# Linear attention and a gated MLP on one core: softmax sums of two more tiles formed in down's rounds, wo's parts loaded and cast later, some loads reordered

## The chip, the cores and the metric

The kernel runs on one core of one Trainium2 chip. The metric is the device time of one execution in microseconds (us); lower is better. The engines are TensorE (PE, with its weight loads as PEld), VectorE (DVE), ScalarE (ACT), GpSimd (POOL) and SyncE (SP), each with a program of its own that it runs in order. SyncE, and ScalarE for a few, also issue DMAs; each DMA issue takes one of eight lanes in turn, so that an issue waits until the eighth DMA before it has landed. Everything is float32.

## The reference

`x` is 2048 x 1024. The output is `x + s * g`: `s` is linear attention with a learned feature map, `g` the silu of a gated MLP, both on the layernorm of `x`.

```python
xn = layernorm(x)
q, k, v = heads(xn @ wqkv)                     # 32 heads of 32
pq, pk  = q @ w_phi, k @ w_phi                 # per head
phi_q   = concat(softmax(pq), softmax(-pq))    # 64 features
phi_k   = concat(softmax(pk), softmax(-pk))
kv      = phi_k.T @ v                          # per head, over all rows
z       = phi_k.sum(rows)
o       = (phi_q @ kv) / (phi_q @ z + 1e-6)
s       = o @ wo
g       = silu((silu(xn @ w1) * (xn @ w3)) @ w2)     # hidden size 3584
out     = x + s * g
```

## The kernel before

Every large product is split twice. Each float32 operand becomes a high and a low part (`split`, L91: a cast on ScalarE, L93, then a subtraction on VectorE, L94), and three passes of matmuls (high x high, high x low, low x high) replace one. On top, blocks of 2 x 2 are multiplied by a scheme with seven products instead of eight (`ORDER`, L60: A11, A12, S2, S1, S3, S4, A22), which accumulate in three PSUM banks a, b and c. A bank is copied out between the products that add onto it, so a later product of the same bank waits for the copy: A11, S2, S3 and A22 share bank b.

The stages follow each other on TensorE:

- Gates and up (PE L667), to about 1117 us: layernorm, w1 and w3, h to DRAM (`h_d`).
- Heads (`heads` L938, PE L947), 1117 to 1450: k and v for the 16 row tiles as 8 pairs, once for each half of the columns (c = 0, 1). The operands `xoA`, `xoS` of a pair are loaded a pair ahead by `reload` (L630): seven loads of 512 KB. After S2 the pair before is added to kv (PE L908, tile `pkv`). Of each pair, `k` is copied from bank b after A11 (ACT L953), d0 after S2 (L964), d1 after S1 (L968); VectorE adds S3 and S4 (L972, L970). Beside this, one part of wo (128 x 512) is loaded (`wo_raw`, L1202), split (`wo_half`) and stored (`wo_d`, L1208) per pair by `wo_split`, at numbered steps j of the pair. Only TensorE's order is written by hand here; the other engines' orders come from the tile scheduler.
- Queries (c = 2; PE L1021), 1450 to 1602: phi_q, stored as `e_d` in DRAM.
- Down (PE L1420), 1602 to 2140: 56 rounds r, each of seven products (the step of a product is 7r + m), h @ w2 summed over kb = r // 8 into 16 slabs `acc`. Work is hung onto products by a table of steps (`pieces`).
- Output (PE L1564 `po`, L1583 `pm`), 2140 to 2356: for each row tile t, `attend` multiplies phi_q with kv (po), the result is cast to high and low parts (`oT`: ACT L1572, DVE L1573), and two halves of 24 matmuls each multiply it by wo (`wos`, and `late` for two of its 16 parts); then x g (DVE L1591) + x (POOL L1595), and the store (SP L1599).

From the last query pair on, all five engines run in the order in which the code is written.

The denominators of phi_q are needed as a factor on e (`scale`, L1397), before it is transposed (L1400) and used by `attend`. They come from products of e with z on GpSimd (`weighted`, L1333), sums over a head's features on VectorE (`summed`, L1336), a small matmul with `consts` that adds the two halves of features (`us`), and a reciprocal (L1369). For the tiles t < `EARLY` = 4 this happens in down's rounds 18 to 39, in eight parts (a tile's half each) 21 products apart: `load_part` (L1330, into a buffer in `room`), the product 12 products later and the sum 16 later, into `early_z`. For the tiles from 4 on it happens in the output loop, for tile t + 4 at step t: `z_products(t + 4)`, later `z_sums(t + 4, c)`, then `weigh`, `add_pairs`, `invert` and `factors` of t + 3 one step on. `z_sums` stands on VectorE between the subtractions of the two column halves that form oT's low parts:

```python
for c in range(2):
    if count:
        lows[c].pop(0)()
    if t + 4 >= EARLY:
        z_sums(t + 4, c)
```

`load_e` (L1389) loads a tile's e, `load_g` (L1549, L1550) the tile's gates g and its x (`xr`), all on SyncE. `B_LOADS` gives the pair and product of c = 2 at which w2's first eight pieces are loaded.

Of the kernel before, what the change touches and what calls it, by code (L numbers as in the profile page):

```python
# [17 lines left out]
P = 128  # L18
# [3 lines left out]
G = 8  # L22
NKB = NF // 4
EPS = 1e-5
PAD = 32


@with_exitstack
def tile_kernel(ctx: ExitStack, tc: tile.TileContext, x, wkT, wqT, wv, wphi, wo, w1, w3, w2, out):
# [104 lines left out]


    edge = [pool("edge_l", 1), pool("edge_r", 1, side="right")]
    edge[0].tile([P, 112], F, name="edge_l")
    edge[1].tile([P, 120], F, name="edge_r")
    misc = pool("misc", 1)
    small = pool("small", 2)  # L140
# [41 lines left out]
    ident = misc.tile([P, P], F, name="ident")  # L182
    consts = misc.tile([P, P], F, name="consts")
    eps_t = consts[:, 0:1]
    early_z = small.tile([P, 256 + PAD], F, name="early_z", bufs=1)[:, :256]

    def load_x(t, halves):
        for h in range(2):
# [132 lines left out]
        nc.sync.dma_start(raw_b[f], w1[f].rearrange("p (h k) n -> p h (k n)", h=2))  # L321
    for f in range(2):
        b_part(rws[f], f, 1)
    phi_raw = early_z.rearrange("p (g f) -> p g f", f=DH)
# [599 lines left out]

    pkv, out_now = None, []

    def kv_run(first, last, tiles):

        nonlocal pkv
        if first:  # L930
            pkv = ps.tile([P, 512], F, name="pkv", tag="kv", bufs=1)[:, :512 // 2]
            pkv = pkv.rearrange("p (m n) -> p m n", m=4)
            zsum.clear()
        for n, (e, v) in enumerate(tiles):
            z_add(e)
            kv(pkv, first and n == 0, last and n + 1 == len(tiles), e, v)

    def heads(first, last, apart, xo, wb, steps, pend):  # L938

        bank = {}  # L940
        for b, an, bn in ORDER:
            if b not in bank:
                bank[b] = ps.tile([P, 512], F, name=f"bank{b}", tag=f"bk{b}", bufs=BANKS[b])
            n = 0
            for k in range(4):
                for u, w in PASSES:
                    nc.tensor.matmul(bank[b], xo[an][:, u, k], wb[bn][:, w, k], start=an in ("A11", "A12", "S1") and n == 0,  # L947
                                     stop=LAST[b] == an and n == 11, skip_group_check=True)
                    n += 1
            pb, pv = bank[b], bank[b].rearrange("p (h d) -> p h d", d=DH)  # L950
            if an == "A11":
                k0 = work.tile([P, 512], F, name="k0", tag="w")
                nc.scalar.copy(k0, pb)  # L953
            elif an == "A12":
                nc.vector.tensor_add(k0, pb, k0)
                e0 = keys(k0, room_e())
            elif an == "S2":
                if pend:
                    kv_run(*pend)
                    if first:  # L960
                        out_now.extend(kv_out(0, pkv))
                v0 = room_v(0)
                d0 = v0
                nc.scalar.copy(d0, pv)  # L964
            elif an == "S1":
                v1 = room_v(1)
                d1 = v1
                nc.scalar.copy(d1, pv)  # L968
            elif an == "S3":
                nc.vector.tensor_add(d1, pv, d1)  # L970
            elif an == "S4":
                nc.vector.tensor_add(d0, pv, d0)  # L972
            else:
                if apart:
                    kv_run(first, False, [(e0, v0)])
# [104 lines left out]
    def query_heads(i, first, xo, wb, steps):  # L1080

        bank, rho = {}, small.tile([P, 2, 2, 16], F, name="rho")
        for b, an, bn in ORDER:
            pb = query_product(bank, b, an, bn, xo, wb)
            if an in ("A11", "S2", "S1"):
                t = work.tile([P, 512], F, name="q", tag="w")
                nc.scalar.copy(t, pb)
                if an == "A11":
                    q00 = t
                elif an == "S2":  # L1090
                    q01 = t
                else:
                    q11 = t
            elif an == "A12":
                nc.vector.tensor_add(q00, pb, q00)
                early = e_room()
                query_features(i, 0, 0, q00, rho, nc.gpsimd, early[:, 0])
            elif an == "S3":
                nc.vector.tensor_add(q11, pb, q11)
                query_features(i, 1, 1, q11, rho, nc.gpsimd, early[:, 1])  # L1100
            elif an == "S4":
                nc.vector.tensor_add(q01, pb, q01)
                late = e_room()
# [95 lines left out]
    def wo_split(c, k, j, halves):  # L1199
        if j == 0:  # L1200
            halves.append(work.tile([P, 512], F, name="wo_raw", tag="w"))
            nc.sync.dma_start(halves[0], wo[k * P:(k + 1) * P, c * 512:(c + 1) * 512])  # L1202
        elif j == 3:
            halves.extend(work.tile([P, 512], R, name="wo_half", tag="w") for _ in range(2))
            split(halves[1], halves[2], halves[0])
        elif j == 5:
            for u in range(2):
                nc.sync.dma_start(wo_d[c][k][:, u], halves[1 + u].bitcast(F))  # L1208

    in_order(ENG.PE)  # L1210
    B_LOADS = ((1, 5), (2, 5), (3, 5), (4, 5), (5, 2), (5, 5), (6, 2), (6, 5))
    NEXT = ({0: 2, 1: 3, 2: 4, 3: 5, 4: 6}, {0: 2, 1: 3, 2: 4, 3: 5, 6: 6}, {})
    for c in range(3):
        wbn, last = {}, c == 2
# [4 lines left out]
        for pos, i in enumerate(order):  # L1219
            nxt, end = {}, pos + 1 == len(pairs)  # L1220

            def steps():
                halves = []
                for j in range(7):
                    if not last:
                        wo_split(c, pos, j, halves)
                    if j == 0:
                        if pos in (3, 4) and not last:
                            wbn.update(fetch(3 + c, pos - 3))
                        if not end:  # L1230
                            nxt.update(reload(order[pos + 1]))
                    if last and (pos, j) in B_LOADS:
                        m = B_LOADS.index((pos, j))
                        load_b(0, m // 2, (m % 2,))
                    if end and j in NEXT[c]:
                        wbn.update(fetch(3 + c, NEXT[c][j]))
                    if last and pos + 2 == len(pairs) and j == 5:
                        ahead[0] = load_h(0, 0)
                    yield
# [21 lines left out]
        load_b(0, n)  # L1261

    wos, us, ezs = {}, {}, []
    EARLY, KEPT, gs = 4, 6, {}

    def load_wo(k):
        t = ring("wos")
# [3 lines left out]
    def gate(i, j):  # L1271
# [3 lines left out]
            nc.scalar.dma_start(g_d[t], slabs[:, m])  # L1275
        else:
            gs[t] = slabs[:, m]

    def slot_f(name):
        return flat(ring(name).bitcast(F))  # L1280
# [55 lines left out]
        nc.vector.tensor_reduce(of_half(dst, c), by_head(e), axis=AX.X, op=OP.add)  # L1336

    def weigh_early():
        nc.gpsimd.tensor_mul(early_z, early_z, w_all[:, :256])

    def add_early():
        us["early"] = ps.tile([P, 512], F, name="us", tag="kv", bufs=1)
        nc.tensor.matmul(us["early"][:, :256], consts, early_z, start=True, stop=True)

    def invert_early(k):
        u = us.pop("early") if k else us["early"]
        nc.vector.reciprocal(early_z[:, k * P:k * P + P], u[:, k * P:k * P + P])

    def z_products(t):
# [106 lines left out]
        pieces.setdefault(at_, []).append(do)  # L1456

    for n in range(2 * EARLY):
        at_ = 7 * 18 + 21 * n
        piece(at_, lambda n=n: load_part(n))  # L1460
        piece(at_ + 12, lambda n=n: weighted(er, er, n % 2))
        piece(at_ + 16, lambda n=n: summed(early(n // 2), er, n % 2))
    piece(at_ + 17, load_weights)
    piece(at_ + 30, weigh_early)
    piece(at_ + 33, add_early)
    piece(at_ + 35, lambda: invert_early(0))
    piece(at_ + 37, lambda: invert_early(1))
# [10 lines left out]
    for r, new in enumerate(steps):  # L1478
# [6 lines left out]
        if r == 4:  # L1485
# [1 line left out]
            room_z = rwp.tile([P, 2, D], F, name="room", tag="rw")  # L1487
            zb, er = room_z[:, 0], room_z[:, 1]
            w_all = er
        if r == 17:  # L1490
            load_z()
        if end:
            if i == 0:
# [4 lines left out]
                    load_wo(k)  # L1498
            elif 4 < i < 8:
                load_e(i - 4)  # L1500
        parts, bank = first, {}
        if r and new:
            gen2 = second_parts(*parts)
# [41 lines left out]
    def load_g(t):  # L1545
        if t < NT:
            if t not in gs:
                gs[t] = flat(quad("g", F).rearrange("p u k t -> p u (k t)"))
                nc.sync.dma_start(gs[t], g_d[t])  # L1549
            nc.sync.dma_start(xrs[t % 2], x[t * P:(t + 1) * P, :])  # L1550


# [46 lines left out]
        nc.sync.dma_start(out[t * P:(t + 1) * P, cs], gs[t][:, cs])  # L1599

    load_g(0)
    load_e(4)
    for c in range(2):
        attend(0, c, 1)[0]()
    prev, lows = None, []
    for t in range(NT):
        p, last = out_half(t, 0), t + 1 == NT
        if t + 5 < NT:
            load_e(t + 5)
        if 0 < t < 3:  # L1610
            gate(len(pairs) - 1, t - 1)
        for low in lows:
# [12 lines left out]
        if prev:  # L1625
            gate_mul(t - 1, 1, prev)
            gate_add(t - 1, 1, False)
            store_out(t - 1, 1)
        load_g(t + 1)
        gate_mul(t, 0, p)  # L1630
        if t + 3 >= EARLY:
            add_pairs(t + 3)
# [53 lines left out]
```

## Time and profile before

| | us |
|---|---|
| median of 3 runs | 2359.5 (2357.18 to 2361.13) |
| profiled execution, its own time | 2358.1 |
| its span, first to last instruction | 2356.3 |
| TensorE busy | 2325.3 (99%) |
| VectorE busy | 1819.5 (77%) |
| ScalarE busy | 888.9 (38%) |
| GpSimd busy | 255.4 (11%) |
| granted clock, mean | 0.998 |

A row of the timeline gives start and duration in us, the engine and line, the operation with output <- input, the count, and in brackets the idle time of the engine ahead of it with what ended that idle time. Idle time matters on TensorE, whose busy share is 99%; on another engine it costs nothing by itself. "SPq" and "PEld" are SyncE's DMA issues and TensorE's weight loads. A row of the wait list gives the engine and line that waited, what it waited for, the total, the number of times and the longest.

### The profile page before, as it was taken

The page shows a single profiled execution, that of the slowest core. Times are in us where ns is not written, and L with a number is a line of the kernel's source. Part 1 is how long each engine was busy: PE and PEld are TensorE (multiplying, and loading weights), DVE is VectorE, ACT ScalarE, POOL GpSimd, SP SyncE. Part 2 cuts the span into 40 slices and gives each one's busy share as a digit, 9 for nine tenths or more (in the row PEclk, how much of TensorE's full clock was granted, in tenths as well). Part 3 has the DMA queues.
Part 4 walks back from the last instruction along what each step waited for, and adds up shares of the span by engine and source line. Part 5 has one row for each costly group of instructions (what it writes and reads, how often), then busy time and mean ns, then how long its engine had stood idle before and what let it go on. Part 6 is the DMA issues. An engine that isn't in the chain of part 4 may idle for free.

```text
span 2356.3 us, 33840 instructions
## 1 busy us (share of the span) xinstructions
PE 2325.3 (99%) x12734; PEld 1901.6 (81%) x12734; DVE 1819.5 (77%) x2853; ACT 888.9 (38%) x1561; POOL 255.4 (11%) x212
## 2 busy tenths in 40 slices
PE   8999999999999999999999999999999999998999
PEld 6778877788888888888787887888888888886777
DVE  8878788885688888874677777778678888786884
ACT  6445444443345555543222222334433343352000
POOL 1000000000000000000000001331012222112652
PEclk9999999999999999999999999999999999999999
DMA  3456799997778888866978878996543554478863
GB/s 128 160 193 225 245 306 370 342 323 222 244 280 300 301 289 295 292 250 224 366 263 307 284 254 318 343 336 242 172 143 126 194 185 137 176 231 251 224 183 104
DMA packets 301460, 578.84 MB, mean 246 GB/s; under 512 B 24424, under 2 KB 156656, under 8 KB 298608
## 3 DMA queue, kind: packets, MB, share of 16 engines
q1 hardware_dynamic: 294960, 553.60, 69.7%
q10 hardware_dynamic: 6336, 23.07, 2.5%
q8 instruction: 100, 1.64, 0.3%
q14 instruction: 64, 0.52, 0.1%
HBM read 373.69 MB, written 202.91 MB: 245 GB/s over the span
## 4 chain that ended last, share of the span: by engine, by line
PE 91%; DMA 5%; DVE 3%; ACT 1%; SPq 0%; issue 0%; POOL 0%; ACTq 0%; DVEq 0%; POOLq 0%
PE bankb L667 26%; PE bankb L1420 13%; PE bankc L667 13%; PE bankc L1420 6%; PE pm L1583 6%; PE bankb L947 6%; PE banka L667 6%; PE banka L1420 3%; PE bankc L947 3%; PE bankb L1021 3%; PE banka L947 1%; PE bankc L1021 1%; DMA wo_raw<-in_wo 1%; DMA xoA<-xo_d0A 1%; PE po L1564 1%; PE pkv L908 1%
## 5 line engine op out<-in xcount | busy, mean ns | idle before, releaser
L94 DVE TENSOR_TENSOR bo<-rw,bo 128x512 fp32r<-128x512 f32 x329 | 226.1, 688 | 145.3 <-ACT bo L93 144.9
L1420 PE MATMUL bankb<-bo,as 128*128 128x512 f32 x960 | 235.0, 389 | 0.0
L1420 PEld LDWEIGHTS bankb<-bo,as 128*128 128x128 f32 x960 | 180.2, 188 | 37.4
L93 ACT CAST bo<-rw 128x512 fp32r<-128x512 f32 x329 | 202.2, 617 | 19.8 <-DMA wkv_d0B<-w2o 2.6
L990 POOL TENSOR_TENSOR eq<-q,mm 128x512 f32<-128x512 f32 x24 | 25.2, 1051 | 1520.7 <-DVE mm L988 1492.7
L667 PE MATMUL bankb<-op0S,bo 128*128 128x512 f32 x672 | 165.7, 396 | 4.5 <-ACT u L703 2.8
L1583 PE MATMUL pm<-wos,oT 128*128 128x512 f32 x672 | 160.4, 395 | 6.5 <-DVE oT L1573 5.1
L667 PE MATMUL bankc<-op0S,bo 128*128 128x512 f32 x672 | 162.0, 390 | 0.0
L667 PE MATMUL bankb<-op1S,bo 128*128 128x512 f32 x672 | 161.3, 389 | 0.0
L667 PE MATMUL bankc<-op1S,bo 128*128 128x512 f32 x672 | 161.2, 389 | 0.0
L667 PE MATMUL bankb<-op0A,bo 128*128 128x512 f32 x672 | 159.3, 391 | 1.1 <-ACT op0A L766 0.8
L1420 PE MATMUL bankc<-bo,as 128*128 128x512 f32 x624 | 158.5, 389 | 0.2 <-DVE acc L1434 0.2
L667 PE MATMUL bankb<-op1A,bo 128*128 128x512 f32 x672 | 158.1, 390 | 0.0
L667 PEld LDWEIGHTS bankb<-op0S,bo 128*128 128x128 f32 x672 | 125.8, 189 | 37.0 <-issue 5.4
L1583 PEld LDWEIGHTS pm<-wos,oT 128*128 128x128 f32 x672 | 126.1, 189 | 35.9 <-DVE oT L1573 5.9
L667 PEld LDWEIGHTS bankb<-op1A,bo 128*128 128x128 f32 x672 | 125.8, 188 | 28.3 <-DVE u L711 2.1
L667 PEld LDWEIGHTS bankb<-op0A,bo 128*128 128x128 f32 x672 | 125.4, 188 | 27.5 <-ACT op0A L766 1.0
L667 PEld LDWEIGHTS bankc<-op0S,bo 128*128 128x128 f32 x672 | 125.6, 188 | 27.2 <-issue 1.2
L667 PEld LDWEIGHTS bankc<-op1S,bo 128*128 128x128 f32 x672 | 126.2, 188 | 26.2
L667 PEld LDWEIGHTS bankb<-op1S,bo 128*128 128x128 f32 x672 | 126.2, 188 | 26.2
L1420 PEld LDWEIGHTS bankc<-bo,as 128*128 128x128 f32 x624 | 117.1, 188 | 24.9 <-DVE acc L1434 0.6
L1434 DVE TENSOR_TENSOR acc<-bankb,acc 128x512 f32<-128x512 f32 x152 | 102.0, 685 | 29.7 <-PE bankb L1420 29.5
(291 smaller groups left out, 4326.0 us busy)
## 6 DMA issues: line engine op xcount, KB each, us to landing
rw<-in_w SPq DMA_DIRECT2D x112, 512.0 KB, 5.5
hr<-h_d SPq DMA_DIRECT2D x56, 512.0 KB, 6.8
h_d<-h SPq DMA_DIRECT2D x108, 256.0 KB, 5.7
xoS<-xo_d0S SPq DMA_DIRECT2D x44, 512.0 KB, 5.0
xoS<-xo_d1S SPq DMA_DIRECT2D x44, 512.0 KB, 5.2
xoA<-xo_d0A SPq DMA_DIRECT2D x33, 512.0 KB, 6.8
xoA<-xo_d1A SPq DMA_DIRECT2D x33, 512.0 KB, 5.5
e_d<-eq ACTq DMA_DIRECT2D x32, 512.0 KB, 6.9
```

The costliest lines, as they stand in the source:

```text
L93: nc.scalar.copy(hi, src)
L94: (by or nc.vector).tensor_sub(lo, src, hi.bitcast(F))
L667: nc.tensor.matmul(bank[b], bos[tb, f][bn][:, w, k], ao[an][:, u, k], start=first and n == 0, stop=LAST[b] == an and n == 11, skip_group_c ...
L908: nc.tensor.matmul(pkv[sl, m], v[:, 4 * m + h], e[:, :, 4 * m + h], start=first and m == 0, stop=last, skip_group_check=True)
L947: nc.tensor.matmul(bank[b], xo[an][:, u, k], wb[bn][:, w, k], start=an in ("A11", "A12", "S1") and n == 0, stop=LAST[b] == an and n == 11, ...
L990: eng.tensor_sub(e[:, 0], p3, mm[:, 0, :].unsqueeze(2).to_broadcast([P, 16, DH]))
L1021: nc.tensor.matmul(bank[b], xo[an][:, u, k], wb[bn][:, w, k], start=an in ("A11", "A12", "S1") and n == 0, stop=LAST[b] == an and n == 11, ...
L1420: nc.tensor.matmul(bank[b], t[:, u, pos + k], bos[kb, bn, k][:, w], start=first and n == 0, stop=LAST[b] == an and n == 5, skip_group_chec ...
L1434: nc.vector.tensor_add(c, pb, c)
L1564: nc.tensor.matmul(po[32 * j:32 * j + 32, a, k, :64 * n], kvs[sl, j, c, k], et[sl, :, :, 4 * k + j], start=True, stop=True, skip_group_che ...
L1583: nc.tensor.matmul(p, oTs[t, h][:, a, k], wos[c, 4 * h + k][:, b], start=n == 0, stop=n == 3 * ND - 1)
```

## The change

- `EARLY` becomes 6. `early_z` grows from 256 to 384 columns (the edge tile gets smaller by as much), the parts become twelve, beginning at step 7 x 6 instead of 7 x 18 with the same spacing and the same end; z is loaded at round 5 instead of 17. There are three reciprocals of `early_z` instead of two, and one product with `consts` over 384 columns. The output loop forms the sums of the tiles from 6 on only.
- Tile 0's gates are loaded among wo's loads (`load_gate(0)` in the step after the last round), not behind them. `load_e(4)` moves from ahead of `attend(0)` into step 0 of the loop, `load_e(5)` behind the loads of tile 1's gates.
- A part of wo is split at j = 4 instead of 3 and stored at j = 6 instead of 5, and its load is issued behind the step's operand loads.
- Seven of the eight loads of `B_LOADS` come later within c = 2.
- In the last pair of c = 1, the tile's part of z is added in the following query pair (`late_z`).

```diff
-    edge[0].tile([P, 112], F, name="edge_l")
+    edge[0].tile([P, 16], F, name="edge_l")
...
-    early_z = small.tile([P, 256 + PAD], F, name="early_z", bufs=1)[:, :256]
+    early_z = small.tile([P, 384], F, name="early_z", bufs=1)
...
         for n, (e, v) in enumerate(tiles):
-            z_add(e)
+            if late:
+                late_z.append(e)
+            else:
+                z_add(e)
...
             pb = query_product(bank, b, an, bn, xo, wb)
+            if late_z:
+                z_add(late_z.pop())
...
-        elif j == 3:
+        elif j == 4:
             halves.extend(work.tile([P, 512], R, name="wo_half", tag="w") for _ in range(2))
             split(halves[1], halves[2], halves[0])
-        elif j == 5:
+        elif j == 6:
...
-    B_LOADS = ((1, 5), (2, 5), (3, 5), (4, 5), (5, 2), (5, 5), (6, 2), (6, 5))
+    B_LOADS = ((3, 5), (4, 2), (4, 5), (5, 2), (5, 5), (6, 1), (6, 3), (6, 5))
...
                 for j in range(7):
-                    if not last:
-                        wo_split(c, pos, j, halves)
                     if j == 0:
                         if pos in (3, 4) and not last:
                             wbn.update(fetch(3 + c, pos - 3))
                         if not end:
                             nxt.update(reload(order[pos + 1]))
+                    if not last:
+                        wo_split(c, pos, j, halves)
...
-    EARLY, KEPT, gs = 4, 6, {}
+    EARLY, KEPT, gs = 6, 6, {}
...
+    def load_gate(t):
+        gs[t] = flat(quad("g", F).rearrange("p u k t -> p u (k t)"))
+        nc.sync.dma_start(gs[t], g_d[t])
...
     for n in range(2 * EARLY):
-        at_ = 7 * 18 + 21 * n
+        at_ = 7 * 6 + 21 * n
...
-    piece(at_ + 35, lambda: invert_early(0))
-    piece(at_ + 37, lambda: invert_early(1))
+    for k in range(EARLY // 2):
+        piece(at_ + 35 + k, lambda k=k: invert_early(k))
...
-        if r == 17:
+        if r == 5:
             load_z()
...
             elif 4 < i < 8:
                 load_e(i - 4)
+            elif i == 8:
+                load_gate(0)
...
     load_g(0)
-    load_e(4)
...
         if t + 5 < NT:
-            load_e(t + 5)
+            load_e(t + 5 if t else 4)
...
         load_g(t + 1)
+        if t == 0:
+            load_e(5)
```

Three places in the engines' programs. First SyncE's at the change from the first to the second pair of c = 0 (`h_d` are the last stores of h; the seven xo loads are the second pair's, `xoA` for A11, A12 and A22, `xoS` for the four sums). Before:

```order
L623 DMA h_d_6_70<-h_9827 128x4x128
L1202 DMA wo_raw<-in_wo 128x512
L630 DMA xoA_9861<-xo_d0A_87 128x1024
L630 DMA xoA_9863<-xo_d0A_88 128x1024
L630 DMA xoS_9865<-xo_d0S_89 128x1024
L630 DMA xoS_9867<-xo_d0S_90 128x1024
L630 DMA xoS_9869<-xo_d0S_91 128x1024
L630 DMA xoS_9871<-xo_d0S_92 128x1024
L630 DMA xoA_9873<-xo_d0A_93 128x1024
```

and changed:

```order
L622 DMA h_d_6_70<-h_9827 128x4x128
L629 DMA xoA_9859<-xo_d0A_87 128x1024
L629 DMA xoA_9861<-xo_d0A_88 128x1024
L629 DMA xoS_9863<-xo_d0S_89 128x1024
L629 DMA xoS_9865<-xo_d0S_90 128x1024
L629 DMA xoS_9867<-xo_d0S_91 128x1024
L629 DMA xoS_9869<-xo_d0S_92 128x1024
L629 DMA xoA_9871<-xo_d0A_93 128x1024
L1208 DMA wo_raw<-in_wo 128x512
```

The load of wo's first part went from ahead of the seven loads to behind them.

Second, VectorE's program at the start of the output loop, from the product with g of tile 0's first half on (`own<-ez` are the sums of tiles 4 and 5, `acc<-acc,early_z` the scales of e, each followed by its transposes). Before:

```order
L1591 TENSOR_TENSOR g<-pm,g 128x512
L1573 TENSOR_TENSOR oT<-po,oT 128x2x4x64
L1336 TENSOR_REDUCE own<-ez 128x2x16
L1573 TENSOR_TENSOR oT<-po,oT 128x2x4x64
L1336 TENSOR_REDUCE own<-ez 128x2x16
L1573 TENSOR_TENSOR oT<-po,oT 128x2x4x64 x2
L1397 TENSOR_TENSOR acc<-acc,early_z 128x1024 x2
L1400 STREAM_TRANSPOSE acc<-acc 128x1024 x2
L1591 TENSOR_TENSOR g<-pm,g 128x512 x2
L1369 RECIPROCAL own<-us 128x64
L1336 TENSOR_REDUCE own<-ez 128x2x16 x2
L1397 TENSOR_TENSOR acc<-acc,own 128x1024 x2
```

and changed:

```order
L1602 TENSOR_TENSOR g<-pm,g 128x512
L1584 TENSOR_TENSOR oT<-po,oT 128x2x4x64 x4
L1407 TENSOR_TENSOR acc<-acc,early_z 128x1024 x2
L1410 STREAM_TRANSPOSE acc<-acc 128x1024 x2
L1602 TENSOR_TENSOR g<-pm,g 128x512 x2
L1407 TENSOR_TENSOR acc<-acc,early_z 128x1024 x2
L1410 STREAM_TRANSPOSE acc<-acc 128x1024 x2
L1602 TENSOR_TENSOR g<-pm,g 128x512 x2
```

The four subtractions that form oT stand together, with no sum between or ahead of them, and tile 4's scale takes its factors from `early_z`.

Third, ScalarE's program in the first two pairs of c = 0 (`ACTIVATE ev` is the exponential of a key's features, `k_9993` the second pair's k, `bankb` and `bankc` the copies of d0 and d1). Before:

```order
L968 COPY ev<-bankc 128x512
L93 CAST wo_half<-wo_raw 128x512
L115 ACTIVATE ev<-ev 128x1024
L953 COPY k_9993<-bankb 128x512
L964 COPY ev<-bankb 128x512
L93 CAST wo_half<-wo_raw 128x512
```

and changed:

```order
L972 COPY ev<-bankc 128x512
L114 ACTIVATE ev<-ev 128x1024
L92 CAST wo_half<-wo_raw 128x512
L957 COPY k_9993<-bankb 128x512
L968 COPY ev<-bankb 128x512
L972 COPY ev<-bankc 128x512
```

The first part's cast moved behind the exponential of the first pair's A22 and now stands directly ahead of the second pair's copy of k.

More of the change, by code (lines that the diff above doesn't have):

```diff
@@ L24 @@
 EPS = 1e-5
-PAD = 32
 @with_exitstack
@@ L323, in tile_kernel @@
         b_part(rws[f], f, 1)
-    phi_raw = early_z.rearrange("p (g f) -> p g f", f=DH)
+    phi_raw = early_z[:, :256].rearrange("p (g f) -> p g f", f=DH)
     nc.sync.dma_start(phi_raw, wphi)
@@ L925, in tile_kernel, with kv_run @@
     pkv, out_now = None, []
-    def kv_run(first, last, tiles):
+    late_z = []
+    def kv_run(first, last, tiles, late=False):
         nonlocal pkv
@@ L974, in heads @@
                 if apart:
-                    kv_run(first, False, [(e0, v0)])
+                    kv_run(first, False, [(e0, v0)], True)
                     e0 = v0 = d0 = None
@@ L1338, in weigh_early @@
     def weigh_early():
-        nc.gpsimd.tensor_mul(early_z, early_z, w_all[:, :256])
+        nc.gpsimd.tensor_mul(early_z, early_z, w_all[:, :64 * EARLY])
     def add_early():
         us["early"] = ps.tile([P, 512], F, name="us", tag="kv", bufs=1)
-        nc.tensor.matmul(us["early"][:, :256], consts, early_z, start=True, stop=True)
+        nc.tensor.matmul(us["early"][:, :64 * EARLY], consts, early_z, start=True, stop=True)
     def invert_early(k):
-        u = us.pop("early") if k else us["early"]
+        u = us.pop("early") if 2 * k + 2 == EARLY else us["early"]
         nc.vector.reciprocal(early_z[:, k * P:k * P + P], u[:, k * P:k * P + P])
@@ L1547, in load_g @@
             if t not in gs:
-                gs[t] = flat(quad("g", F).rearrange("p u k t -> p u (k t)"))
-                nc.sync.dma_start(gs[t], g_d[t])
+                load_gate(t)
             nc.sync.dma_start(xrs[t % 2], x[t * P:(t + 1) * P, :])
```

## The prediction, made before the changed kernel had run

> **What bounds the kernel now.** I read the page's busy times and its chain first, then the list of what TensorE waited for, then the timeline of the stages that hold the waits.
>
> ```profile
> span 2356.3 us, 33840 instructions
> PE 2325.3 (99%) x12734; PEld 1901.6 (81%) x12734; DVE 1819.5 (77%) x2853; ACT 888.9 (38%) x1561; POOL 255.4 (11%) x212
> PE 91%; DMA 5%; DVE 3%; ACT 1%; SPq 0%; issue 0%; POOL 0%; ACTq 0%; DVEq 0%; POOLq 0%
> ```
>
> TensorE is busy for 2325.3 of 2356.3 us, so the kernel is its matmuls, and only 31 us of idle time, plus whatever runs at a lower clock, can be won without removing matmuls. The change removes almost none. The question is therefore which of the 31 us go and which new ones come. The waits by cause (total, times, longest):
>
> ```profile
> PE pm L1583 <- DVE oT L1573: 5.1, 2, 4.9
> PE pm L1583 <- DVE g L1591: 1.5, 1, 1.5
> PE pkv L908 <- DVE ev L121: 1.3, 1, 1.3
> PE bankb L947 <- DMA xoA<-xo_d0A: 0.9, 1, 0.9
> PE bankc L1420 <- DVE acc L1434: 0.2, 1, 0.2
> ```
>
> The largest outside the start is one 4.9-us wait of the output stage (L1583). The down rounds (L1420) wait for 0.2 us in all. The head stage (L947, L908) has small ones. These three places are what the change touches.
>
> **Output stage: the stall that goes.** Timeline around it (start, duration, then in brackets the idle time ahead and what ended it):
>
> ```profile
> 2153.77 6.21 PE L1583 MATMUL pm<-wos,oT 128*128 128x512 f32 x26
> 2160.59 4.65 POOL L1333 TENSOR_TENSOR ez<-acc,room 128x1024 f32<-128x1024 f32 x2 [27.64 <-DMA acc<-e_d]
> 2162.96 1.22 DVE L1336 TENSOR_REDUCE own<-ez 128x32 f32<-128x1024 f32 x1 [9.12 <-POOL ez L1333]
> 2164.10 0.68 DVE L1573 TENSOR_TENSOR oT<-po,oT 128x512 fp32r<-128x512 f32 x1
> 2164.84 3.35 PE L1583 MATMUL pm<-wos,oT 128*128 128x512 f32 x7 [4.85 <-DVE oT L1573]
> 2167.61 6.04 DVE L1397 TENSOR_TENSOR acc<-acc,early_z 128x1024 f32<-128x1024 f32 x2
> 2170.16 4.93 PE L1583 MATMUL pm<-wos,oT 128*128 128x512 f32 x21
> 2176.56 5.05 PE L1583 MATMUL pm<-wos,oT 128*128 128x512 f32 x21 [1.46 <-DVE g L1591]
> 2179.69 2.34 DVE L1397 TENSOR_TENSOR acc<-acc,own 128x1024 f32<-128x1024 f32 x2
> 2183.34 1.15 PE L1564 MATMUL po<-acc,kvs 64*32 64x128 f32 x64 [0.35 <-DVE acc L1400]
> 2184.42 0.96 PE L1583 MATMUL pm<-late,oT 128*128 128x512 f32 x3
> ```
>
> TensorE ends its run of 26 at 2159.98 and needs the low half oT. VectorE could form it at once, but its program has the sum of tile 4 (own<-ez) ahead of it, that waits for GpSimd's product, and that for the load of e_d, which lands at 2160.59. After the change tiles 4 and 5 have their sums from down's rounds: neither product nor sum stands here, and VectorE goes straight to oT (second order piece above).
>
> The gain is worked out over the stretch 2159.98 to 2184.42, where the loop first has its regular step: 24.44 us. In it run 58 pm matmuls. From the row of 21 in 4.93 us, less one matmul of 0.39 us for the pipeline's end, a matmul starts every (4.93 - 0.39)/20 = 0.227 us, so 58 take 13.2; the one po takes 1.15. That is 14.4 needed, and 24.44 - 14.4 = **10.0 us** lost. The parts: 4.85 for oT, 1.46 for g behind VectorE's slow scale (6.04 against 2.34 for the same two instructions later), the two small us matmuls and what surrounds them about 1.1, the rest a lowered clock:
>
> ```profile
> 2160.00:2162.00 2.00, 0.00 (x0) 0.00 (x0) 0.00 (x0) 0.00 (x0) 1.41 (x1) 1.00 1.04 214
> 2162.00:2164.00 2.00, 0.00 (x0) 0.00 (x0) 1.04 (x1) 0.00 (x0) 2.00 (x2) 0.59 1.01 265
> 2166.00:2168.00 2.00, 2.00 (x7) 1.52 (x6) 2.00 (x4) 0.00 (x0) 1.90 (x3) 0.50 0.35 138
> 2168.00:2170.00 2.00, 2.00 (x9) 1.66 (x8) 2.00 (x1) 0.00 (x0) 2.00 (x2) 0.70 0.76 208
> 2170.00:2172.00 2.00, 2.00 (x11) 1.63 (x10) 2.00 (x2) 0.00 (x0) 2.00 (x1) 1.00 1.02 220
> ```
>
> (Columns: busy time and count of PE, PEld, DVE, ACT, POOL, then the granted clock, the DMA share and GB/s.) The clock falls about 2.4 us into the stall and is back about 4 us after TensorE restarts at 2164.84; half speed for 4 us costs 2. Bounds on the gain: 10.0 if nothing is late next, 0 if another wait takes the place. What is late next are loads: this stage's DMA is near full (shares of 1.0 above), tile 4's e now goes behind xr, and tile 1's g ahead of tile 5's e. Tile 4's e is needed for its scale, which VectorE by its new order reaches at about 2163 (an estimate from the order and the durations above), and the last strip of both tiles was in by 2160.59 with the same bytes ahead of it; tile 4 alone is earlier. Margin some 3 us, so I take 10.0, and put the loss of it into a rival.
>
> **Head stage: a stall that comes.** wo's first part was loaded ahead of the second pair's operands, now behind all seven of them (first order piece), and its cast stands before `COPY k` of that pair on ScalarE (third piece).
>
> ```profile
> 1137.32 0.32 SPq L630 DMA_DIRECT2D xoA<-xo_d0A  x1
> 1137.92 0.62 ACT L93 CAST wo_half<-wo_raw 128x512 fp32r<-128x512 f32 x1 [6.56 <-DMA wo_raw<-in_wo]
> 1139.68 3.03 PE L947 MATMUL bankb<-op2B,xoA 128*128 128x512 f32 x12 [0.91 <-DMA xoA<-xo_d0A]
> 1142.75 0.59 ACT L953 COPY k<-bankb 128x512 f32<-128x512 f32 x1
> 1145.27 2.88 PE L947 MATMUL bankb<-op2T,xoS 128*128 128x512 f32 x12
> 1105.00:1160.00 55.00, 54.09 (x297) 44.27 (x297) 24.54 (x36) 11.32 (x17) 0.00 (x0) 1.00 1.01 405
> ```
>
> The DMA engines are saturated here (share 1.01). A small gain: the two xoA loads no longer stand behind wo_raw, so the matmul at 1139.68 waits up to 0.91 us less, with its weight load about -1.1. The cost: wo_raw takes the issue slot of 1137.32. The transfers of two issues nearby, KB and us to landing, are
>
> ```profile
> xoA<-xo_d0A SPq DMA_DIRECT2D x1, 512.0 KB, 9.9
> wo_raw<-in_wo SPq DMA_DIRECT2D x1, 256.0 KB, 5.8
> ```
>
> 9.9 us is the load issued at 1137.32 itself, 5.8 the old wo_raw of 1132. By the first, with as many bytes ahead of it, wo_raw lands at 1147.2; by the second at 1143.1. I take the first: same time, same backlog. Then the cast ends at 1147.85, `COPY k` (0.59) at 1148.45, and the matmuls that add onto the bank it reads start at about 1148.65 instead of 1145.27: **+3.4**, an idle stretch of 4.4 us (TensorE would be free at 1144.2). By the second the copy ends by 1144.4, and nothing is lost: -1.1. Bounds -1.1 and +3.4, before the clock.
>
> The clock: in the output stall it fell after 2.4 us of idling and the restart cost 2.0. A stall of 4.4 us is past that point, so I add **+2.0**; bounds 0 and 2.0. [...]
>
> In the next pair VectorE now has its subtraction from bankb later in its order, so the tile ev is ready for a whole run of 64:
>
> ```profile
> 1168.38 0.65 PE L908 MATMUL pkv<-ev 128*32 128x64 f32 x32
> 1170.31 0.65 PE L908 MATMUL pkv<-ev 128*32 128x64 f32 x32 [1.28 <-DVE ev L121]
> ```
>
> The two halves and the wait go from 1168.38 to 1170.96, 2.58; a whole run elsewhere takes 1.10, so **-1.5** (bounds -1.5 and 0). In the second pass's pair 1 a transposition of kv is queued behind the keys' subtractions; about **+0.4** (bounds 0 and 1). From pair 4 on the three orders are as before. Head stage: -1.1 is inside the +3.4; 3.4 + 2.0 - 1.5 + 0.4 = +4.3.
>
> **Down: four more parts.** Each part is 4 loads on SyncE, one GpSimd product and one VectorE sum.
>
> ```profile
> L1333 POOL TENSOR_TENSOR room<-room x8: 2846/2849/2849, 1789.7 to 1989.7; 128x1024 f32<-128x1024 f32 x8
> SPq L1330 <- DVE early_z L1336: 51.7, 6, 9.0
> 1600.00:1700.00 100.00, 100.00 (x443) 82.84 (x442) 70.41 (x127) 47.83 (x86) 7.34 (x6) 1.00 0.63 220
> 1700.00:1800.00 100.00, 100.00 (x443) 82.84 (x442) 77.11 (x125) 38.60 (x76) 18.96 (x21) 1.00 0.46 149
> ```
>
> 4 x 2.85 us on GpSimd, busy for 7 to 19 us in a hundred, and 4 x 1.22 on VectorE, busy for 70 to 77: both are hidden behind TensorE's full rounds. SyncE waits up to 9.0 us for a room already in rounds 18 to 39, and TensorE did not notice (0.2 us in all). So 0, and without that cover the price is the last rival. The early us matmul grows from 256 to 384 columns: half of one full matmul's time more, in two passes about **+0.2**. w2's first loads, later: one of eight moves past other loads, its due time is far off; 0.
>
> [...]
>
> **Sum**, against the profiled execution of 2358.1 us: -10.0 + 4.3 + 0.2 = -5.5, so 2352.6. The median of the runs is 1.4 above that execution; on it the forecast is 2359.5 - 5.5 = **2354.0 us**.
>
> **Rivals.**
> *No cold restart, or no stall in the head stage.* If the clock holds through the 4.4 us: -7.5, 2352.0. If wo_raw lands in 5.8 us: -10.0 - 1.1 - 1.5 + 0.4 + 0.2 = -12.0, 2347.5. For: two loads nearby took such different times. Against: the saturated share and the 9.9 us of the very slot.
> *The output gain is half lost.* Tile 4's e, or g and xr of tile 1, come late, as loads share a full DMA: a new wait of 2 to 4 us, with the clock's 2 us where it is long. Gain 4 to 7 instead of 10: 2357 to 2360. For: VectorE waited for g in this very stage, in the trace's row
>
> ```profile
> 2152.56 0.69 DVE L1591 TENSOR_TENSOR g<-pm,g 128x512 f32<-128x512 f32 x1 [4.02 <-DMA g<-g_d]
> ```
>
> but TensorE did not. Against: the bytes are the same, and GpSimd's demand is gone.
> *Slower: SyncE is held in down's early rounds.* SyncE issues in order. If a part's load waits for its room in rounds 6 to 17, the operand loads of the next round stand behind it. It decides where that wait (9.0 at the longest so far) exceeds their lead. One such stall of 9.0 us with a cold restart of 2.0 turns -5.5 into +5.5: 2365. For: those rounds carry more DMA (0.63 against 0.46) and ScalarE work (47.83 against 38.60). Against: the 0.2 us above.
> *The change doesn't do what it says.* VectorE meets another late producer ahead of oT, the stall stays, and only the head stage's cost shows: +4.5, 2364. Against: the order has nothing left there but oT.
>
> **How the numbers follow.** Forecast 0.40; no cold restart or no stall 0.25; half the gain 0.20; slower by SyncE 0.10; stall stays 0.05. What a measurement of this kernel tells from no change is about 0.2%, 4.7 us. The forecast lies only 0.8 beyond it, so I count 0.28 of its 0.40 as faster; with the 0.25 of the first rival and 0.05 of the second that is 0.58. The slower cases give 0.13, the rest, 0.29, is no difference. The range reaches from the first rival's 2347.5 to 2362, which takes in all of the half gain and leaves out the slower cases.
>
> **What would show it.** Right: no wait of the L1583 matmuls for oT around 2160, clock 1.00 throughout, and the step 2159.98 to 2184.42 at about 14.5 us; in the head stage one wait of 4 to 5 us ahead of the matmuls after `COPY k` of pair 1, led back to wo_raw, perhaps with a clock of 0.5 behind it; no new wait in L1420. Wrong: `COPY k` of pair 1 near 1142, or a new wait for e_d or g in the output stage, or TensorE idle in down.

## The result and the profile after

| | before | changed |
|---|---|---|
| median of 8 runs each, us | 2357.1 (2356.2 to 2361.1) | 2351.6 (2349.6 to 2352.8) |
| profiled execution, own time (span) | 2358.1 (2356.3) | 2350.9 (2349.1) |

The medians lie 5.5 us apart. The ratio, which is formed from all sixteen runs and not from the medians, is 0.9973, with a 95% interval of 0.9962 to 0.9984: 6.4 us less at a time of 2357, with an interval from 3.8 to 9.0. The forecast was 5.5 less. Its 2354.0 us started from a median of 2359.5 of three runs; the eight have 2357.1.

First the page of the changed kernel, then its list of TensorE's waits (total, times, longest):

```profile
span 2349.1 us, 33851 instructions
PE 2323.7 (99%) x12730; PEld 1900.2 (81%) x12730; DVE 1821.3 (78%) x2852; ACT 888.8 (38%) x1561; POOL 257.0 (11%) x208
```

```profile
PE bankb L951 <- ACT k L957: 3.5, 1, 3.5
PE bankb L951 <- DVE ev L974: 1.3, 2, 0.7
PE pm L1594 <- DVE oT L1584: 0.2, 1, 0.2
PE bankc L1430 <- DVE acc L1444: 0.2, 1, 0.2
```

The 4.9 us for oT and the 1.5 us for g have gone from the output stage, the 1.3 us for `pkv` and the 0.9 us for xoA from the head stage. A new wait of 3.5 us for the copy of k stands there. In down TensorE waits 0.2 us as before, though SyncE waits longer in all for the rooms of the parts:

```profile
SPq L1340 <- DVE early_z L1346: 84.7, 10, 9.0
```

Where the time went is read off the timelines by the start of each stage's first matmul (1119.57, 1284.72, 1450.18, 1606.70 and 2140.87 before; 1119.01, 1286.94, 1452.64, 1609.12 and 2143.96 changed) and the span. The round times that the description of the kernel gives for the first head and the first down matmul, 1117 and 1602, are 2.6 and 4.7 us too early.

| stage, us | before | changed | difference | predicted |
|---|---|---|---|---|
| start, gates and up | 1119.57 | 1119.01 | -0.6 | 0 |
| heads, c = 0 | 165.15 | 167.93 | +2.8 | +3.9 |
| heads, c = 1 | 165.46 | 165.70 | +0.2 | +0.4 |
| queries | 156.52 | 156.48 | 0.0 | 0 |
| down | 534.17 | 534.84 | +0.7 | +0.2 |
| output | 215.43 | 205.14 | -10.3 | -10.0 |

The timeline of the changed kernel's output stage, where the stall had been:

```profile
2156.88 7.80 PE L1594 MATMUL pm<-wos,oT 128*128 128x512 f32 x33
2158.12 1.89 DVE L1584 TENSOR_TENSOR oT<-po,oT 128x512 fp32r<-128x512 f32 x3 [3.36 <-ACT oT L1583]
2159.92 2.79 DVE L1407 TENSOR_TENSOR acc<-acc,early_z 128x1024 f32<-128x1024 f32 x2
2164.52 1.52 PE L1594 MATMUL pm<-late,oT 128*128 128x512 f32 x6
2165.88 9.68 PE L1594 MATMUL pm<-wos,oT 128*128 128x512 f32 x42
2166.92 0.69 DVE L1602 TENSOR_TENSOR g<-pm,g 128x512 f32<-128x512 f32 x1 [1.35 <-DMA g<-g_d]
2177.26 0.97 PE L1594 MATMUL pm<-late,oT 128*128 128x512 f32 x3
```

TensorE runs on through what had been a run of 26, a stall and a run of 7 (x33, no bracket), because the three subtractions that form oT follow ScalarE's cast at once. VectorE now waits for a DMA (1.35 us for g), and TensorE does not. The step that the prediction measured at 24.44 us (from the end of the 26th matmul, here 2156.88 + 6.21 = 2163.09, to the start of the row of 3 at 2177.26) now takes 14.17. That is 10.3 us less, so the whole gain of the output stage lies in it.

The timeline of the head stage, c = 0, pairs 1 and 2, with the granted clock of the stretch (busy time and count of PE, PEld, DVE, ACT, POOL, then the clock, the DMA share, GB/s):

```profile
1136.81 0.42 SPq L1208 DMA_DIRECT2D wo_raw<-in_wo  x1
1140.79 2.88 PE L951 MATMUL banka<-op2B,xoA 128*128 128x512 f32 x12
1146.02 0.62 ACT L92 CAST wo_half<-wo_raw 128x512 fp32r<-128x512 f32 x1 [4.19 <-DMA wo_raw<-in_wo]
1146.55 0.58 ACT L957 COPY k<-bankb 128x512 f32<-128x512 f32 x1
1147.18 4.54 PE L951 MATMUL bankb<-op2T,xoS 128*128 128x512 f32 x12 [3.50 <-ACT k L957]
1151.64 1.10 PE L907 MATMUL pkv<-ev 128*32 128x64 f32 x64
1152.67 3.06 PE L951 MATMUL bankc<-op2T,xoS 128*128 128x512 f32 x12
```

```profile
1144.00:1146.00 2.00, 0.00 (x0) 0.00 (x0) 1.97 (x3) 0.00 (x0) 0.00 (x0) 1.00 1.03 416
1146.00:1148.00 2.00, 0.82 (x2) 0.73 (x3) 1.35 (x4) 1.10 (x2) 0.00 (x0) 0.76 0.86 347
1148.00:1150.00 2.00, 2.00 (x6) 1.52 (x6) 1.27 (x2) 0.00 (x0) 0.00 (x0) 0.50 1.12 271
1150.00:1152.00 2.00, 2.00 (x31) 1.41 (x33) 0.00 (x0) 0.00 (x0) 0.00 (x0) 0.89 0.66 160
```

This is the chain that was foretold: the part of wo is issued at 1136.81 and there at 1146.0, the cast is the next thing on ScalarE, the copy of k is behind it, and the twelve matmuls that add onto the copied bank stand still for 3.5 us; then they take 4.54 us instead of 2.88 at half the clock.

### The profile page after: what moved, and what is told of

Read it like the earlier page. It is cut to its first block, busy times and chain, and to the rows that moved or that the text cites. A ratio compares the mean times of both kernels' runs of the same rounds, so it can differ in the third digit from the quotient of the medians.

```text
span 2349.1 us, 33851 instructions
## 1 busy us (share of the span) xinstructions
PE 2323.7 (99%) x12730; PEld 1900.2 (81%) x12730; DVE 1821.3 (78%) x2852; ACT 888.8 (38%) x1561; POOL 257.0 (11%) x208
## 4 chain that ended last, share of the span: by engine, by line
PE 89%; DMA 6%; DVE 2%; ACT 1%; issue 0%; POOL 0%; SPq 0%; ACTq 0%; POOLq 0%
PE bankb L666 26%; PE bankc L666 13%; PE bankb L1430 13%; PE bankc L1430 6%; PE bankb L951 6%; PE banka L666 6%; PE pm L1594 5%; PE banka L1430 3%; PE bankc L951 3%; PE bankb L1025 2%; PE banka L951 1%; DMA acc<-e_d 1%; DMA wo_raw<-in_wo 1%; PE bankc L1025 1%; DMA h_d<-h 1%; PE pkv L907 1%
## 5 line engine op out<-in xcount | busy, mean ns | idle before, releaser
L717 ACT ACTIVATE h<-bankb 128x512 f32<-128x512 f32 x56 | 33.5, 598 | 236.8 <-PE bankb L666 236.8
```

What stands on the lines that cost most here:

```text
L717: nc.scalar.activation(h1, bank["b"], AF.Silu)
```

## The experiments

Unless said otherwise each edit is made to the changed kernel; stages are cut as in the table, from each run's profiled execution. Ratios are to the kernel before, which ran on the same chip. The times of one kernel's executions spread over 2 to 7 us, so where a profiled execution lies at the edge of its runs, the median decides.

**The load of wo's parts ahead again** (cast still at product 4):

```diff
                 for j in range(7):
+                    if not last:
+                        wo_split(c, pos, j, halves)
                     if j == 0:
...
-                    if not last:
-                        wo_split(c, pos, j, halves)
```

> The changed kernel with the load of each of wo's parts issued ahead of the step's operand loads again, its cast still at product 4. Theory (the wait ahead of the second pair's S2 comes from the load's place behind seven operand loads): no wait for the copy of k, clock 1.00 from 1140 to 1154, the head stage (first L951 matmul to the first query matmul) back from 333.6 to 330.6 us, the output stage (first po to the end) still 205 us, the span near 2346. Rival (the cast's later product makes the wait): the wait of 3.5 us and the cold restart stay, head stage 333.6, span near 2349.

Median 2345.9, ratio 0.9951 (0.9936 to 0.9965). c = 0 took 164.8 us, c = 1 165.2, the output stage 204.9, the span 2345.7. Its waits in the head stage:

```profile
PE bankb L951 <- DVE ev L974: 1.3, 2, 0.7
PE pkv L907 <- DVE ev L120: 1.3, 1, 1.3
PE bankb L951 <- DMA xoA<-xo_d0A: 0.5, 1, 0.5
```

The wait for k is gone, the two small waits of the kernel before (for `pkv` and for xoA) are back, and the first row stands in all three kernels. So the place of the load makes the new wait, and this version beats both kernels. Its median is 5.8 us below the changed kernel's; between the two profiled executions 3.1 us of that lie in c = 0, and 1.9 are spread over the later stages.

**The cast's product back to 3**, load still behind (`j == 4` and `j == 6` back to 3 and 5):

> The changed kernel with the cast back at product 3 and the store at product 5, the load still behind the operand loads; ScalarE's and VectorE's programs come out row for row as in the changed kernel. Theory: the same wait of 3.5 us for the copy of k, the time that of the changed kernel. [...] Rival (the cast's product matters): no wait.

Median 2350.0 (2346.8 to 2352.2), ratio 0.9967 (0.9956 to 0.9978), c = 0 169.0 us, and

```profile
1148.81 4.57 PE L951 MATMUL bankb<-op2T,xoS 128*128 128x512 f32 x12 [3.50 <-ACT k L957]
```

The same wait: in this stage the tile scheduler orders ScalarE, and moving the cast by a product in the code moved nothing there (the trace has the same rows in the same order on ScalarE, VectorE and GpSimd as the changed kernel's). "wo's parts cast one product later" is by itself no edit; its companion, the later load, is.

**wo_split's change alone, on the kernel before:**

> The kernel before with only the change to wo_split (load behind the operand loads, cast at product 4). Theory: TensorE waits 3.5 us for the copy of k in pair 1 of c = 0, the next pair's wait of 1.28 goes, c = 0 takes 166.3 us if the clock holds and 168 if it falls, instead of 165.15; output stage 215 as before; median 1 to 3 us above the kernel before. Rival (the wait needs the other edits): c = 0 at 165.2, no wait for k.

Median 2361.9, ratio 1.0015 (1.0006 to 1.0024): 3.6 us slower than the runs of the kernel before beside it. c = 0 took 168.6 us, the output stage 216.5.

```profile
PE pm L1583 <- DVE oT L1573: 6.0, 2, 5.8
PE bankb L947 <- ACT k L953: 3.5, 1, 3.5
```

The head stage's loss needs none of the other edits.

**The sums alone, on the kernel before** (`EARLY` 6, the parts from step 7 x 6, z at round 5, the wider `early_z` and its product; no load moved, `wo_split` and `B_LOADS` old):

```diff
...
-    EARLY, KEPT, gs = 4, 6, {}
+    EARLY, KEPT, gs = 6, 6, {}
...
-        at_ = 7 * 18 + 21 * n
+        at_ = 7 * 6 + 21 * n
...
```

> The kernel before with the sums of tiles 0 to 5 in down's rounds from 6 on (EARLY 6), and none of the other edits. Theory (VectorE's sum of tile 4 ahead of oT is the whole stall): no wait of 4.9 us for oT, clock 1.00, output stage 205 to 206 instead of 215.4 us, head stage 330.6 as before, down +0.2 for the wider product, span 2346 to 2347. Rival (the earlier gates of tile 0 carry a good part, since VectorE waits 4.02 us for them and is late afterwards): output stage 208 to 212, with waits of TensorE for g or oT left.

Median 2349.7 (2348.6 to 2353.6), ratio 0.9967 (0.9955 to 0.9978), 8.9 us below the runs of the kernel before beside it. The profiled execution is the slowest of its six (2353.6), and its output stage took 209.5 us: the wait at 2160 is gone there too, but a step later VectorE's scale again ran beside GpSimd's product, and TensorE waited for g:

```profile
2186.71 5.73 POOL L1333 TENSOR_TENSOR ez<-acc,room 128x1024 f32<-128x1024 f32 x2
2187.30 6.23 DVE L1397 TENSOR_TENSOR acc<-acc,early_z 128x1024 f32<-128x1024 f32 x2
2196.44 6.65 PE L1583 MATMUL pm<-wos,oT 128*128 128x512 f32 x21 [1.89 <-DVE g L1591]
```

By the profile alone the rival of the loads looks half right; by the median the sums carry the gain. The next two runs part them.

**The reordered loads alone, on the kernel before** (tile 0's gates in the step after the last round, e of tiles 4 and 5 later):

> The kernel before with only the reordered loads: tile 0's gates among wo's, tile 4's e behind xr, tile 5's behind tile 1's gates. Theory: VectorE's wait of 4.02 us for g goes, but the sum of tile 4 still waits for its e, so TensorE's wait for oT stays at 4 to 6 us with the cold restart, output stage 214 to 217, span 2355 to 2358. Rival (the gates carry a good part): output stage 208 to 212.

Median 2358.5, ratio 0.9999 (0.9990 to 1.0008). The profiled execution is the fastest of ten (2353.5); its output stage took 211.6 us:

```profile
2161.22 1.22 DVE L1340 TENSOR_REDUCE own<-ez 128x32 f32<-128x1024 f32 x1 [10.28 <-POOL ez L1337]
2163.10 3.35 PE L1588 MATMUL pm<-wos,oT 128*128 128x512 f32 x7 [3.83 <-DVE oT L1578]
```

VectorE's wait for g has gone, the sum still stands ahead of oT, and TensorE still waits. The output stage of this one execution lies where the rival had it, but the other nine executions took 2357.5 to 2360.0 and the median is that of the kernel before: alone the loads are worth nothing that can be measured. In the same profile c = 0 took 167.0 us, though nothing of the head stage was edited, so a stage's time from a single execution is uncertain by some 2 us.

**The changed kernel with its loads in the old order:**

> The changed kernel with its loads in the old order: tile 0's gates behind wo's parts, e of tiles 4 and 5 together ahead of the loop. Theory: the output stage stays within 1 us of 205, since VectorE has slack of some microseconds; span 2349 to 2350. Rival: the old order costs part of the gain, output stage 207 or more, with VectorE's wait of about 4 us for g passed on to oT.

Median 2350.5 (2349.5 to 2352.3), ratio 0.9970 (0.9958 to 0.9981), output stage 206.0 us. VectorE waits for g on arrival, and TensorE, by the rows below, does not notice:

```profile
2156.36 7.79 PE L1592 MATMUL pm<-wos,oT 128*128 128x512 f32 x33
2156.86 0.69 DVE L1600 TENSOR_TENSOR g<-pm,g 128x512 f32<-128x512 f32 x1 [5.76 <-DMA g<-g_d]
2157.47 2.48 DVE L1582 TENSOR_TENSOR oT<-po,oT 128x512 fp32r<-128x512 f32 x4
```

So with the sums gone VectorE has slack enough for either order of the loads.

One difference stays open. The run with wo's load ahead again and the run with the sums alone have the same rows in the same order on ScalarE, VectorE and GpSimd, yet their medians are 3.8 us apart (2345.9 and 2349.7), and the slowest execution of the first (2347.5) is faster than the fastest of the second (2348.6). They differ in the order of the output stage's loads, in w2's loads and in when wo's parts are stored. Taking back the first of these, here, or the second, in the next run, cost the changed kernel nothing; what makes the 3.8 us was not found.

**w2's first loads at their old products** (`B_LOADS` back):

> The changed kernel with w2's first loads at their old products. In the changed kernel's second down round TensorE's weight loads wait 0.24 and 0.43 us for the high and low part of h, whose load (hr) comes 2.8 us late instead of 1.1. Theory (w2's loads, moved to the end of the query stage, delay that load): the waits go, down 534.4 instead of 534.8 us, everything else as in the changed kernel, span 0.4 lower, too little for the median. Rival (chance, or the parts of z): down stays at 534.8 or the query stage gets longer by as much.

My theory of this run fell. Median 2352.0, ratio 0.9974 (0.9965 to 0.9983); down took 535.3 us and the weight loads waited longer, not less:

```profile
PEld bankb L1430 <- ACT af L92: 0.7, 1, 0.7
PEld bankb L1430 <- DVE af L93: 0.4, 1, 0.4
```

Over the profiles of all these kernels ScalarE's wait for that load of h is 1.1 to 3.4 us, and it is 2.5 in the run with the reordered loads alone, which has neither the sums nor the later loads of w2. The longest, 3.4, stands in the run with the sums alone, where down took 1.2 us more than before and not the 0.2 that was expected. It varies from one execution to the next; what makes it vary was not found. In the changed kernel the weight loads waited for it for 0.2 and 0.4 us.

**First and last part of wo apart.** The first run left room: the waits of pairs 1 and 2, and those at the end of each pass, where the copy of d1 is held behind the last part's cast. Two versions followed. In the first the first part is loaded ahead of the operands, the last part of each pass a pair earlier (`pre` keeps it until its own pair), w2's loads at their old products:

```diff
...
+                    if c == pos == 0 == j:
+                        wo_split(c, pos, j, halves)
...
-                    if not last:
+                    if not last and c + pos + j:
                         wo_split(c, pos, j, halves)
+                    if not last and pos + 2 == len(pairs) and j == 5:
+                        wo_split(c, pos + 1, 0, pre.setdefault((c, pos + 1), []))
```

> The changed kernel with three edits: the first of wo's parts is loaded ahead of the second pair's operands, the last part of each pass one pair earlier, and w2's first loads at their old products. Theory: no wait for k in pair 1, the next pair's wait of 1.28 gone as in the changed kernel (c = 0 1.4 us below the kernel before), the waits at the end of both passes (0.2 to 0.7 us each, with the copy held behind the cast of the last part) gone, 1.2 per pass: c = 0 162.5, c = 1 164.3, output stage 205, span 2341 to 2343, some 7 us below the changed kernel. Rival (the pass's end waits for its operands, not for the part of wo): c = 0 163.8, c = 1 165.5, span 2344 to 2345.

Median 2345.3, ratio 0.9949 (0.9935 to 0.9962). c = 1 fell to 163.8 us as expected, and no wait is left at the passes' ends; c = 0 took 166.1, because the wait for the keys of pair 2 was longer than ever:

```profile
PE pkv L907 <- DVE ev L120: 1.9, 1, 1.9
PE bankb L951 <- DMA xoA<-xo_d0A: 1.0, 1, 1.0
```

The changed kernel had lost this wait through its late load, which gave VectorE another order; with the load ahead, an order close to the old one came back. That I had not seen when I wrote the expectation. The second version has no part of wo in the first pair at all, and two in the sixth (`more` is the second of them):

```diff
...
-                    if not last:
+                    if not last and c + pos:
                         wo_split(c, pos, j, halves)
+                    if not c and pos == 5:
+                        wo_split(c, 0, j, more)
+                    if not last and pos + 2 == len(pairs) and j == 5:
+                        wo_split(c, pos + 1, 0, pre.setdefault((c, pos + 1), []))
```

> The changed kernel with wo's first part moved from the first pair of c = 0 to the sixth, beside that pair's own part, and the last part of each pass loaded one pair earlier. In the run with the first part ahead of the operand loads, 1.0 us for xoA and 1.9 us for the keys ev (with a cold restart) were left in pairs 1 and 2. Theory: without any part of wo in the first pair neither stands there, VectorE reaches ev earlier than in the kernel before, no wait at the passes' ends: c = 0 161.5 to 163, c = 1 164, output stage 205, span 2340 to 2342, median 2342 to 2344. Rival (the two parts in one pair make a wait of their own for a copy behind the casts, or the wait for ev stays since VectorE's subtraction from bank b still stands ahead of the keys): c = 0 165 or more, span 2343 to 2345.

Median 2342.9 (2342.0 to 2346.9), ratio 0.9939 (0.9925 to 0.9952): the fastest of all. c = 0 took 162.0 us, c = 1 163.9, the output stage 204.9, the span 2340.2. In the head stage one wait is left:

```profile
PE pkv L907 <- DVE ev L120: 0.6, 1, 0.6
```

## Why the prediction was right

- **The output stage's gain: right in mechanism and size.** 10.0 foretold, 10.3 measured, all of it in the step from which the 10.0 was worked out (24.44 us before, 14.17 now, some 14.5 foretold). The sums alone bring 8.9 by the median, the loads alone bring nothing, and the changed kernel keeps the gain with its loads in the old order. The margin that the prediction gave the loads was real: they could be moved either way.
- **The head stage's stall: right in mechanism, over-sized.** Place, cause and chain are as foretold, and the run with the load ahead shows the cause. The term was +4.3 and measured +3.0. Of the step "+3.4" 2.5 came (measured from the stage's start), since the part landed 9.2 us after its issue, not 9.9, and the restart followed the copy more closely. "+2.0" for the clock came as 1.7: the step from those matmuls to the next bank's is 5.49 us against 3.84. "-1.5" in pair 2 was 1.5 (2.51 us from the first `pkv` matmul to the next bank's before, 1.03 changed), "+0.4" in the second pass 0.2.
- **The rival "no cold restart" is not decided by the kernel.** The same stall of 3.5 to 3.6 us stands in five of the kernels' profiles. The clock fell in four of them and held in the one with the loads in their old order (last section), whose edit lies behind the head stage. Fall or no fall was worth 1.7 us in the changed kernel. The 0.25 covered this and, with it, the early landing of wo_raw in 5.8 us, which did not come.
- **Down: +0.2 was right for what it named.** The wider product costs 0.22 (0.81 against 0.59 us for the pair). The rest of the 0.7 goes with the late load of h, which no edit explains. GpSimd's four more products and SyncE's waits cost nothing. SyncE's waits for a room rose from 51.7 to 84.7 us, but none is longer than the 9.0 us of before, and the rival in which SyncE is held did not come: TensorE waits 0.2 us in down as before.
- **w2's later loads: 0 was right**, with no effect by the medians (2352.0 with the old products, 2351.6 with the new).
- **The sum.** -5.5 foretold; -7.2 between the two profiled executions, of which 0.6 lies ahead of the head stage, where the change does nothing; -5.5 between the medians. That this last agrees to a tenth is luck, with an interval of 3.8 to 9.0 and a head stage that was over-sized by 1.3. The mechanism is better borne out by the edits made alone on the kernel before: -8.9 for the sums, 0.0 for the loads and +3.6 for wo_split add up to -5.3.

## What to carry to other kernels

On an engine that runs in order, an instruction that waits for something late holds everything that is queued behind it: the sum of a tile needed much later held oT (TensorE waited 4.85 us), and the cast of a part needed much later held k (3.50 us). Take such instructions out of the stage with no slack (the sums into down, the first part of wo into the sixth pair) rather than shifting them by a step. Where a scheduler orders an engine, move the load, look at the order that comes out, and test each edit alone: here one part of the change gave nine or ten microseconds and another took three or four back.

## What the runs showed of the hardware

**Stalls of 1.89 to 4.9 us came with a fall of the clock, one of 3.6 us came without; it stayed low for 3.4 or 6.8 us.** Within a slice of 2 us the mean clock gives the moment of a change between 1.0 and 0.5. In the changed kernel the fall comes at 1147.0 (0.76 in the slice from 1146) and the return at 1150.4 (0.89 in that from 1150): 3.4 us. In the stall of the kernel before, shown with the prediction, it falls at 2162.4 and returns at 2169.2, 6.8 us, twice as long. The stall with the old order of loads, 3.6 us and so as long as that of the changed kernel, shows no fall:

```profile
1144.00:1146.00 2.00, 1.46 (x7) 0.88 (x5) 1.93 (x3) 0.00 (x0) 0.00 (x0) 1.00 1.02 414
1146.00:1148.00 2.00, 0.00 (x0) 0.00 (x0) 1.72 (x3) 0.13 (x1) 0.00 (x0) 1.00 1.04 422
1148.00:1150.00 2.00, 0.98 (x4) 0.85 (x5) 1.45 (x3) 0.97 (x2) 0.00 (x0) 1.00 0.79 315
```

and in the run with the sums alone a wait of 1.89 us came with one:

```profile
2194.00:2196.00 2.00, 0.55 (x3) 0.13 (x1) 2.00 (x3) 0.00 (x0) 0.00 (x0) 1.00 0.63 126
2196.00:2198.00 2.00, 1.56 (x4) 1.27 (x5) 2.00 (x4) 0.00 (x0) 1.54 (x3) 0.64 0.01 3
2198.00:2200.00 2.00, 2.00 (x7) 1.51 (x6) 2.00 (x3) 0.00 (x0) 1.27 (x2) 0.51 0.72 182
```

It falls at 2196.6, and 1.9 of the 3.4 us ahead of that were idle. So the 2.4 us that the prediction calls "that point" were not needed for a fall.

The records of the clock in the traces of the kernel before and of the changed one give the two low stretches as 6.827 and 3.413 us, and within each of the two traces all changes lie whole multiples of 3.4133 us (2102.61 / 616) apart, such as 616 between 59.76 and 2162.37 in the kernel before and 319 between 58.18 and 1147.03 in the changed one. In the trace of the stall without a fall the clock falls in these two slices, near the start and behind the last matmul,

```profile
60.00:62.00 2.00, 1.61 (x7) 1.29 (x8) 2.00 (x5) 0.86 (x2) 0.00 (x0) 0.94 0.00 0
2348.00:2349.00 1.00, 0.00 (x0) 0.00 (x0) 0.00 (x0) 0.00 (x0) 0.00 (x0) 0.85 0.00 0
```

at 61.78 and 2348.71, which is 670 times that length; counted on from 61.78 by the same length (an estimate), one such moment is 1147.22. The stall, 1145.45 to 1149.02, has 1.77 idle us ahead of it and 1.80 behind it. Of the 3.4133 us ahead of the falls at 2162.37 in the kernel before and 1147.03 in the changed one, 2.39 and 3.36 were idle. What makes the clock fall, and in how many executions a stall of 3.5 us goes without it, these runs do not show: of the five profiles with that stall, one had no fall.

How long it stayed low differed too. In the changed kernel TensorE ran again from 1147.18, 0.14 us behind the fall, and the clock was low for 3.4 us. In the kernel before 2.5 of the 3.4 us behind the fall were idle, and it was low for 6.8; in the run with the reordered loads alone it was also low from 2162.4 to 2169.2, though TensorE ran again from 2163.1 and only 0.7 us behind the fall were idle:

```profile
2166.00:2168.00 2.00, 2.00 (x8) 1.61 (x7) 2.00 (x2) 0.00 (x0) 1.34 (x1) 0.50 0.77 243
```

**Halves of a scale that began beside an operation of GpSimd took 1.66 to 3.42 us, the others 1.2.** 6.04 us for the two halves in the kernel before and 6.23 in the run with the sums alone, against 2.35 by themselves. In the kernel before GpSimd's products end at 2169.23 and 2172.57 and the two halves of the scale at 2170.31 and 2173.65, each 1.08 us later, nearly their length alone (1.2). In the profiles of the kernel before and the changed one 13 halves began while an operation of GpSimd ran; each ended 1.08 to 1.09 us after that operation. The other 51 took 1.20 to 1.22 us, among them one in the changed kernel, at 2189.26, beside which a product began 0.14 us later. After the two slow scales TensorE waited for g, 1.46 us in the kernel before and 1.89 in the run with the sums alone, so where VectorE has no slack for these 4 us, the order of GpSimd's products matters.
